# Two more dummy products, a constant made on VectorE, and one query transfer instead of two, in the opening of a fused attention and gated-FFN kernel

## Chip, cores, metric

One Trainium2 chip, one core. The metric is device time in microseconds, the median of several executions. The span in a profile is about 1.7 us shorter than the time of the same run.

## The reference, cut to what matters

```python
# attention: 4 batches, 8 heads, 768 tokens, head 64; window of +-15 tokens
k_sum = k.reshape(B, H, nb, 32, D).max(axis=3)       # one key per block of 32
v_sum = v.reshape(B, H, nb, 32, D).mean(axis=3)      # one value per block: "block means"
scores = [window scores | q . k_sum * scale + log(32)]
x = softmax(scores) @ [v | v_sum]                    # -> 3072 tokens x 512
# gated FFN with a gated residual
ffn = (gelu(x @ w_gate) * (x @ w_val)) @ w_out
out = x + sigmoid(x @ w_res) * ffn
```

## The kernel before

The work goes in eight units of 384 tokens. The opening: the first unit's keys and queries are loaded, turned on TensorE (PE), scored and normalised, while the FFN weights stream in behind them. Only the touched parts are shown.

```python
nc.vector.memset(warm[:], 0.0)
nc.vector.memset(ident[:], 0.0)
...
nc.vector.memset(bmean[:], 1.0 / BLK)                # block-mean constant, BLK = 32
...
nc.sync.dma_start(out=kf[:], in_=...)                # keys of pair 0, f32
nc.sync.dma_start(out=qf[:], in_=...)                # queries of pair 0, f32
load_tokens(kt, k, 0, 0, S, 2, 4)                    # GpSimd queue, casts on the way
select(ident[:], ALU.not_equal, 1.0, 0, -1, 1)
load_tokens(qa, q, 0, 0, TU, 2, 4)
for h in (4, 6):
    load_tokens(kt, k, 0, 0, S, h, h + 2)
    load_tokens(qa, q, 0, 0, TU, h, h + 2)
select(maskt[0:96], ...); select(maskt[0:96], ...)
load_values(0, NC); load_values(0, 0)
select(bias_t[96:128, :], ...)
for c in range(1, NC):
    load_values(0, c)
select(bmean[:], ALU.is_ge, 0.0, 32 * (NB + 94) - WIN, -32, 1)
select(bmean[:], ALU.is_ge, 0.0, 31 + WIN - 32 * (NB + 94), 32, -1)
for c in range(6):                                   # six pieces of each gate weight
    if c == 5:
        load_tokens(qb, q, 0, TU, S, 0, H)           # queries of the second unit
    nc.gpsimd.dma_start(out=w_gate[:, :, sl], in_=wg_src[:, :, sl])
    nc.gpsimd.dma_start(out=w_val[:, :, sl], in_=wv_src[:, :, sl])
...
def keep_warm(n, wp=None):                           # dummy products, result unused
    for i in range(n):
        nc.tensor.matmul(wp[:], warm[:, 0:128], warm[:], start=True, stop=True)
...
keep_warm(8, s1[0])
nc.scalar.copy(kt[:, 0]..., kf[:, 0])                # cast of the first keys
nc.vector.tensor_copy(kt[:, 1]..., kf[:, 1])
nc.vector.tensor_copy(qa[:, 0:2]..., qf[:])
t = k_first(0)                                       # 16 turns on PE, then an ACT copy
q_step(qa, 0, 0, TU, 0, *MM, nc.vector.tensor_copy)  # 8 turns
keep_warm(2, s1[0])
...
t = k_first(1)
q_step(qa, 0, 0, TU, 1, *MM)
k_first_rest(*t)                                     # VectorE: block maxima and copies
s = mask_into(s_tiles())
keep_warm(2, s1[0])
s_step(0, 0, st, s)                                  # first scores
```

The softmax here doesn't subtract the row's maximum and nothing guards it: scores larger than these inputs give would overflow.

Of the kernel before, what the change touches and what calls it, by code (L numbers as in the profile page):

```python
# [11 lines left out]
ALU = mybir.AluOpType  # L12
# [3 lines left out]
def kernel(  # L16
# [11 lines left out]
    nc = tc.nc  # L28
    B, H, S, D = q.shape
    assert (B, H, S, D) == (4, 8, 768, 64)  # L30
    BLK, WIN = 32, 16
    NB = S // BLK
# [9 lines left out]
    TU = S // 2  # L42
# [23 lines left out]
    ident = const.tile([128, 128], BF16, name="ident")  # L66
# [3 lines left out]
    bmean = const.tile([128, NB - 2 + 128], BF16, name="bmean")  # L70
# [14 lines left out]
    def token_tile(lo, hi, name):  # L85
        j = (hi - lo) // PP
        return qk1.tile([PP, H, j, D], BF16, tag=name, name=name)

    def load_tokens(t, src, b, lo, hi, h0, h1):
        j = (hi - lo) // PP  # L90
        nc.gpsimd.dma_start(
            out=t[:, h0:h1].rearrange("p h j d -> p h (j d)"),
            in_=src[b, h0:h1, lo:hi].rearrange("h (p j) d -> p h (j d)", j=j),
        )

    def load_values(b, c):

        lo, hi = (max(0, c * 128 - WIN), c * 128 + 128 - WIN) if c < NC else (S - WIN, S)
        dst = vext[b % 2][0 if c else WIN:128, 2 * c, :, 0:D] if c < NC else vext[b % 2][64:64 + WIN, NT - 1, :, 0:D]
        nc.gpsimd.dma_start(out=dst, in_=v[b, :, lo:hi, :].rearrange("h p d -> p h d"))  # L100
# [3 lines left out]
    with tc.manual_schedule():  # L104
# [13 lines left out]
        def select(ap, op, fill, base, step, cm):  # L118
            nc.gpsimd.affine_select(out=ap, in_=ap, compare_op=op, fill=fill, base=base,
                                    pattern=[[step, ap.shape[-1]]], channel_multiplier=cm)  # L120
# [2 lines left out]
        nc.vector.memset(ident[:], 0.0)  # L123
        nc.vector.memset(bias_t[:], 0.0)
        nc.vector.memset(bias_t[96:128, :], logblk)
        nc.vector.memset(bmean[:], 1.0 / BLK)
        nc.vector.memset(maskt[:], 1.0)
        vext_consts(0)
        kw_consts(0)
# [2 lines left out]
        kt, qa, qb = token_tile(0, S, "k0"), token_tile(0, TU, "qa"), token_tile(TU, S, "qb")  # L132
# [5 lines left out]
        load_tokens(kt, k, 0, 0, S, 2, 4)  # L138
        select(ident[:], ALU.not_equal, 1.0, 0, -1, 1)
        load_tokens(qa, q, 0, 0, TU, 2, 4)  # L140
        for h in (4, 6):
            load_tokens(kt, k, 0, 0, S, h, h + 2)
            load_tokens(qa, q, 0, 0, TU, h, h + 2)
        select(maskt[0:96], ALU.is_ge, 0.0, -1, -1, 1)
        select(maskt[0:96], ALU.is_ge, 0.0, 2 * WIN - 1, 1, -1)
        load_values(0, NC)
# [1 line left out]
        select(bias_t[96:128, :], ALU.is_ge, -30000.0, NB - 1, 0, -1)  # L148
        for c in range(1, NC):
            load_values(0, c)  # L150
        select(bmean[:], ALU.is_ge, 0.0, 32 * (NB + 94) - WIN, -32, 1)
        select(bmean[:], ALU.is_ge, 0.0, 31 + WIN - 32 * (NB + 94), 32, -1)

        wg_src = moe_w_gate.rearrange("(ko ki) f -> ki ko f", ki=128)
        wv_src = moe_w_val.rearrange("(ko ki) f -> ki ko f", ki=128)
# [61 lines left out]
        def q_step(src, b, lo, hi, hp, pool, tag, copy=nc.scalar.copy):  # L217
            tp = turn_pair(src, hp, pool, tag)
            copy(qT[b % 2][hp][:, lo:hi].rearrange("d (p j) -> d p j", j=tp.shape[2]), tp)
# [12 lines left out]
        def k_first_rest(tp, kw):  # L232
            ks = work.tile([128, NB], BF16, tag="ks", name="ks")
            nc.vector.tensor_reduce(out=ks[:], in_=tp.rearrange("d j (n w) -> d n j w", w=4),
                                    axis=mybir.AxisListType.XY, op=ALU.max)
            nc.vector.tensor_copy(kw[:, 0:HT, BLK0:BLK0 + NB], ks.unsqueeze(1).to_broadcast([128, HT, NB]))
            nc.vector.tensor_copy(kw[:, 1:HT, 0:WIN], kw[:, 0:HT - 1, OWN + QT - WIN:OWN + QT])
            nc.vector.tensor_copy(kw[:, 0:HT, POST:POST + WIN], kw[:, 1:HT + 1, OWN:OWN + WIN])
# [44 lines left out]
        def vsum_out(b, vs, h0, h1, copy):  # L283
            copy(vsum[b % 2][96:128, h0:h1, 0:D],
                 vs[96:128, h0 * D:h1 * D].rearrange("p (h d) -> p h d", d=D))

        def v_spread(b, c0, c1, part, copy=nc.vector.tensor_copy):

            V = vext[b % 2].rearrange("p (c e) h d -> p c e h d", e=2)
            if part == 0:  # L290
                copy(V[0:64, c0:c1, 1, :, 0:D], V[64:128, c0:c1, 0, :, 0:D])
            else:
                hi = min(c1, NC - 1)
                copy(V[64:96, c0:hi, 1, :, 0:D], V[0:32, c0 + 1:hi + 1, 0, :, 0:D])
# [10 lines left out]
        def s_tiles(two=None):  # L305
            if two:
                return [pool.tile([128, 512], F32, tag=tag, name="s1") for pool, tag in two]
            return ps_s.tile([128, 2, 512], F32, tag="s", name="s")

        def mask_into(s):  # L310
            two = isinstance(s, list)
            for hh in range(2):
                nc.tensor.matmul((s[hh] if two else s[:, hh])[:, 0:TU].rearrange("p (t q) -> p t q", t=HT), ident[:],
                                 nmask.unsqueeze(1).to_broadcast([128, HT, QT]),
                                 start=True, stop=False, skip_group_check=True)
            return s
# [128 lines left out]
        def keep_warm(n, wp=None):  # L445
            if wp is None:
                wp = ps_mm.tile([128, 512], F32, tag="mm", name="wp")
            for i in range(n):
                nc.tensor.matmul(wp[:], warm[:, 0:128], warm[:], start=True, stop=True)  # L449
# [18 lines left out]
        st = new_unit()  # L468
        nc.scalar.activation(pre[:], bias_t[0:1, :], AF.Exp)
        s1 = s_tiles((AO, TT))  # L470
        keep_warm(8, s1[0])
        nc.scalar.copy(kt[:, 0].rearrange("p j d -> p (j d)"), kf[:, 0])
        nc.vector.tensor_copy(kt[:, 1].rearrange("p j d -> p (j d)"), kf[:, 1])
        nc.vector.tensor_copy(qa[:, 0:2].rearrange("p h j d -> p h (j d)"), qf[:])
# [5 lines left out]
        t = k_first(1)  # L480
        q_step(qa, 0, 0, TU, 1, *MM)
        k_first_rest(*t)
        s = mask_into(s_tiles())
        keep_warm(2, s1[0])
        s_step(0, 0, st, s)
# [30 lines left out]
        vsum_sum(0, *MM, (5,), vs, first=False, last=True)  # L516
        keep_warm(1, wp)
        vsum_out(0, vs, 0, 2, nc.vector.tensor_copy)
        vsum_out(0, vs, 2, 8, nc.scalar.copy)
        for hp in range(NP):  # L520
            av_part(0, hp, st, blocks=True)
# [10 lines left out]
        for u in range(NU):  # L532
            b, half = u // 2, u % 2
            nb = b + 1
            n = u + 1
# [107 lines left out]
            if u == 1:  # L643
                k_rest(kW[1][3], nc.scalar.copy)
                v_spread(1, 0, HT // 2, 0)
                v_spread(1, 0, HT // 2, 1, nc.scalar.copy)
                end_step(u, st, 0)
                vs = vsum_sum(1, *SS, last=True)
                vsum_out(1, vs, 0, H, nc.scalar.copy)
                for hp in range(2):  # L650
                    vsum_bc(1, hp, 0, HT)
# [68 lines left out]
```

## Time and profile before

| | before |
|---|---|
| median of the first 3 runs (lowest, highest) | 257.66 us (257.52, 258.19) |
| the profiled run itself | 258.93 us, span 257.2 |
| PE busy | 97% of the span |
| first gate product of the first unit | 22.48 us |

The lines that carry the reading are in the prediction below.

In a timeline row the columns are start and duration in us, engine, line, operation, output<-inputs, shape, and in brackets the idle time before it and what ended that. Line numbers of the changed kernel are about ten higher from the middle of the file on (the dummies' L449 becomes L458).

### The profile page before, as it was taken

The page shows a single profiled execution, that of the slowest core. Times are in us where ns is not written, and L with a number is a line of the kernel's source. Part 1 is how long each engine was busy: PE and PEld are TensorE (multiplying, and loading weights), DVE is VectorE, ACT ScalarE, POOL GpSimd, SP SyncE. Part 2 cuts the span into 40 slices and gives each one's busy share as a digit, 9 for nine tenths or more (in the row PEclk, how much of TensorE's full clock was granted, in tenths as well). Part 3 has the DMA queues.
Part 4 walks back from the last instruction along what each step waited for, and adds up shares of the span by engine and source line. Part 5 has one row for each costly group of instructions (what it writes and reads, how often), then busy time and mean ns, then how long its engine had stood idle before and what let it go on. Part 6 is the DMA issues. An engine that isn't in the chain of part 4 may idle for free.

```text
span 257.2 us, 5751 instructions
## 1 busy us (share of the span) xinstructions
PE 250.6 (97%) x2240; PEld 139.8 (54%) x2240; DVE 172.6 (67%) x397; ACT 142.2 (55%) x249; POOL 103.5 (40%) x143
## 2 busy tenths in 40 slices
PE   7989999999999999999999999999999999999993
PEld 3445555566645555456654655556554655555543
DVE  4674975486487876779659768679568853764333
ACT  3584449645597536648683537458683537443310
POOL 7995533792979930028993560020001000010000
PEclk9999999999999999999999999999999999999999
DMA  7999999999999999759999999256003100130012
GB/s 152 157 144 195 197 204 201 149 172 150 128 152 172 168 149 159 109 136 148 162 129 151 183 154 131 49 143 120 0 3 88 82 3 1 33 138 3 0 41 83
DMA packets 118955, 30.46 MB, mean 118 GB/s; under 512 B 106064, under 2 KB 116752, under 8 KB 118928
## 3 DMA queue, kind: packets, MB, share of 16 engines
q0 software_dynamic: 86880, 19.90, 84.9%
q1 hardware_dynamic: 32048, 10.20, 25.2%
q8 instruction: 17, 0.28, 0.4%
q14 instruction: 10, 0.08, 0.1%
HBM read 32.51 MB, written 6.29 MB: 151 GB/s over the span
## 4 chain that ended last, share of the span: by engine, by line
PE 94%; ACT 2%; DMA 1%; DVE 1%; issue 0%; DVEq 0%
PE f L432 24%; PE vv L398 23%; PE g L398 22%; PE r L416 9%; PE gv L545 4%; PE ao L362 4%; PE s L330 3%; DMA kf<-in_k_dram 1%; PE xp L381 1%; PE vs L279 1%; PE s L449 1%; PE tp L226 1%; PE tp L195 1%; ACT kW L228 1%; PE gv L398 1%; PE tp L188 1%
## 5 line engine op out<-in xcount | busy, mean ns | idle before, releaser
L398 PE MATMUL vv<-xT,w_val 128*128 128x384 bf16 x360 | 73.7, 326 | 0.0
L404 ACT ACTIVATE ge<-g 128x384 f32<-128x384 f32 x85 | 41.8, 491 | 51.8 <-DVE gvT L405 25.9
L398 PE MATMUL g<-xT,w_gate 128*128 128x384 bf16 x340 | 69.7, 326 | 0.0
L405 DVE TENSOR_TENSOR gvT<-ge,vv 128x384 bf16<-128x384 f32 x90 | 49.2, 551 | 30.2 <-PE vv L398 26.9
L432 PE MATMUL f<-w_out,gvT 128*128 128x512 bf16 (+2 forms) x312 | 68.0, 363 | 0.0
L443 POOL DMA_DIRECT2D out_dram<-o x15 | 8.3, 552 | 100.4 <-DVE rz L370 81.9
L398 PEld LDWEIGHTS <-w_val 128*128 128x128 bf16 x364 | 35.6, 98 | 23.4
L398 PEld LDWEIGHTS <-w_gate 128*128 128x128 bf16 x344 | 33.3, 98 | 21.6
L432 PEld LDWEIGHTS <-gvT 128*128 128x128 bf16 x312 | 28.5, 98 | 28.9
L422 ACT ACTIVATE th<-r 128x512 f32<-128x512 f32 x24 | 14.2, 602 | 25.8 <-PE r L416 25.8
L437 DVE SCALAR_TENSOR_TENSOR th<-th,f 128x512 f32<-128x512 f32 (+2 forms) x26 | 16.7, 641 | 12.5 <-PE f L432 8.5
L416 PE MATMUL r<-w_res,xT 128*128 128x512 bf16 x96 | 24.4, 380 | 0.0
L175 POOL DMA_DIRECT2D k_sb<-in_k_dram x24 | 19.8, 836 | 11.2 <-DMA w_out<-in_moe_w_out_dram 5.2
L100 POOL DMA_DIRECT2D vext<-in_v_dram x28 | 23.6, 895 | 0.7 <-PE vv L398 0.7
L347 DVE TENSOR_TENSOR P<-P,maskt 128x768 bf16<-128x768 bf16 x28 | 15.5, 557 | 9.5 <-ACT P L336 5.0
L175 POOL DMA_DIRECT2D q_sb<-in_q_dram x24 | 19.8, 875 | 1.8 <-DMA k_sb<-in_k_dram 1.8
L372 DVE TENSOR_TENSOR xn<-ao,rz 128x384 bf16<-128x384 f32 x32 | 17.8, 557 | 1.1
L439 DVE SCALAR_TENSOR_TENSOR o<-th,xn 128x512 f32<-128x512 f32 (+2 forms) x26 | 16.9, 651 | 0.9
L336 ACT ACTIVATE P<-s,bias_t 128x384 bf16<-128x384 f32 x32 | 16.8, 578 | 1.1 <-PE s L330 1.1
L383 ACT COPY xT<-xp 128x384 bf16<-128x384 bf16 x17 | 7.9, 484 | 15.3 <-PE xp L381 15.3
L339 ACT ACTIVATE P<-s,bias_t 128x768 bf16<-128x768 f32 x16 | 14.5, 904 | 2.7 <-PE s L330 2.5
L175 POOL DMA_DIRECT2D v_sb<-in_v_dram x16 | 13.3, 925 | 0.0
(104 smaller groups left out, 248.9 us busy)
## 6 DMA issues: line engine op xcount, KB each, us to landing
out_dram<-o POOLq DMA_DIRECT2D x15, 256.0 KB, 2.4
vext<-in_v_dram POOLq DMA_DIRECT2D x20, 128.0 KB, 7.1
k_sb<-in_k_dram POOLq DMA_DIRECT2D x24, 96.0 KB, 7.8
q_sb<-in_q_dram POOLq DMA_DIRECT2D x24, 96.0 KB, 4.5
out_dram<-o SPq DMA_DIRECT2D x8, 256.0 KB, 3.8
w_gate<-in_moe_w_gate_dram POOLq DMA_DIRECT2D x6, 256.0 KB, 8.8
w_val<-in_moe_w_val_dram POOLq DMA_DIRECT2D x6, 256.0 KB, 9.1
w_out<-in_moe_w_out_dram POOLq DMA_DIRECT2D x3, 512.0 KB, 15.6
```

Of the source, the lines that this page charges most:

```text
L100: nc.gpsimd.dma_start(out=dst, in_=v[b, :, lo:hi, :].rearrange("h p d -> p h d"))
L175: nc.gpsimd.dma_start(out=sb[b][:, h // 2, :, h % 2 * D:h % 2 * D + D], in_=src[b, h].rearrange("(c p) d -> p c d", c=NC))
L336: nc.scalar.activation(P[:, hh].rearrange("p t q -> p (t q)"), s[hh][:, 0:TU], AF.Exp, scale=scale, bias=bias_t[:])
L347: nc.vector.tensor_mul(Pf, Pf, maskt.unsqueeze(1).to_broadcast([128, 2 * HT, QT]))
L372: nc.vector.tensor_mul(xn, ao[:, :, :, 0:D], rz.to_broadcast([128, NSUB, 2, D]))
L398: nc.tensor.matmul(acc[:, 0:TU], w[:, ko, fs], st["xT"][:, ko, :], start=(ko == 0), stop=(ko == KO - 1))
L404: nc.scalar.activation(ge[:], g[:, 0:TU], AF.Gelu)
L405: nc.vector.tensor_mul(gvT[:, fo, :], ge[:], vv[:, 0:TU])
L416: nc.tensor.matmul(r[:], st["xT"][:, ko, ss], w_res[:, ko, :], start=(ko == 0), stop=(ko == KO - 1))
L432: nc.tensor.matmul(st["f", sub][:, 0:c1 - c0], gvT[:, fo, ss], w_out[:, fo, c0:c1], start=(fo == 0), stop=(fo == FO - 1))
L437: nc.vector.scalar_tensor_tensor(th, th, 1.0, f[:, 0:c1 - c0], ALU.add, ALU.mult)
L439: nc.vector.scalar_tensor_tensor(o[:, 0:c1 - c0].rearrange("p (k d) -> p k d", d=128), th.rearrange("p (k d) -> p k d", d=128), 0.5, st["x ...
```

## The change

Two more dummies are to fill the idle time ahead of the first turn, so that PE's clock comes up sooner. Making the constant on VectorE and merging two transfers takes work off GpSimd, which issues the value and weight transfers.

```diff
-        nc.vector.memset(bmean[:], 1.0 / BLK)
+        nc.vector.memset(bmean[:], 0.0)
...
-        for h in (4, 6):
-            load_tokens(kt, k, 0, 0, S, h, h + 2)
-            load_tokens(qa, q, 0, 0, TU, h, h + 2)
+        load_tokens(kt, k, 0, 0, S, 4, 6)
+        load_tokens(qa, q, 0, 0, TU, 4, 8)
+        load_tokens(kt, k, 0, 0, S, 6, 8)
...
-        select(bmean[:], ALU.is_ge, 0.0, 32 * (NB + 94) - WIN, -32, 1)
-        select(bmean[:], ALU.is_ge, 0.0, 31 + WIN - 32 * (NB + 94), 32, -1)
...
+        def mean_consts():
+
+            c = NB + 93
+            with nc.allow_low_precision("sums of one element"):
+                for lo, hi, x in ((0, WIN, c), (WIN, 128 - WIN, c + 1), (128 - WIN, 128, c + 4)):
+                    n = (hi - lo + BLK - 1) // BLK
+                    nc.vector.tensor_reduce(out=bmean[:, x:x + n],
+                                            in_=ident[:, lo:hi].rearrange("p (n w) -> p n w", n=n),
+                                            axis=mybir.AxisListType.X, op=ALU.add)
+            nc.vector.tensor_scalar_mul(bmean[:, c:c + 5], bmean[:, c:c + 5], 1.0 / BLK)
...
-        keep_warm(8, s1[0])
+        keep_warm(10, s1[0])
...
         k_first_rest(*t)
+        mean_consts()
         s = mask_into(s_tiles())
```

## The prediction

> **What bounds the kernel now.** I read the page first: busy shares, then the chain that ended last, then the waits of the tensor engine (PE), then the timelines of the first 40 us engine by engine, because all three parts of the change sit there.
>
> The page's shares and the head of its chain:
>
> ```profile
> PE 250.6 (97%) x2240; PEld 139.8 (54%) x2240; DVE 172.6 (67%) x397; ACT 142.2 (55%) x249; POOL 103.5 (40%) x143
> ...
> PE 94%; ACT 2%; DMA 1%; DVE 1%; issue 0%; DVEq 0%
> ```
>
> PE is busy 97% of a span of 257.2 us. The list of PE's waits over the whole execution adds up to 2.5 us, and 1.3 of that is the start. From about 22.5 us, when the first gate products run, the chain of waits is PE alone without a gap. So only the first 22 us can give or take anything, and what moves there moves the end one for one, unless a later operand is late. I therefore need to know what sets the pace between 1.3 and 22 us. The timeline of PE for that stretch:
>
> ```profile
> 1.27 3.60 PE L449 MATMUL s<-warm 128*128 128x512 bf16 x8 [1.27 <-DVE warm L122]
> 5.20 0.85 PE L226 MATMUL tp<-ident,k 96*64 96x96 bf16 x16 [0.33 <-ACT k L472]
> 5.84 0.52 PE L195 MATMUL tp<-ident,qa 96*64 96x96 bf16 x8
> 6.30 1.03 PE L449 MATMUL s<-warm 128*128 128x512 bf16 x2
> 7.26 0.85 PE L226 MATMUL tp<-ident,k 96*64 96x96 bf16 x16
> 8.36 0.82 PE L313 MATMUL s<-nmask,ident 128*128 128x384 bf16 x2
> 8.98 1.06 PE L449 MATMUL s<-warm 128*128 128x512 bf16 x2
> 9.97 0.50 PE L330 MATMUL s<-qT,kW 64*128 64x64 bf16 x12
> 10.41 0.69 PE L449 MATMUL s<-warm 128*128 128x512 bf16 x2
> 11.36 0.53 PE L226 MATMUL tp<-ident,k 96*64 96x96 bf16 x16
> ```
>
> Columns are start, duration, engine, line, operation. Three things are to be seen. The eight dummy products (L449) end, in pace, at 1.27 + 8 x 0.427 = 4.69 us, and PE then stands idle until the key cast lets the first turn begin at 5.20. Second, the same work has two speeds: sixteen turns of keys occupy 0.85 us at 5.20 and 7.26 but 0.53 us at 11.36, and two dummies take 1.06 us at 8.98 and 0.69 at 10.41. PE runs at half speed until about 10.6 us and at full speed after. The page's row of granted clock shows 9 in every slice, so it does not show this; the durations do. Third, in the slow stretch the chain of waits is PE nearly without a break:
>
> ```profile
> 5.20 0.85 PE tp L226 x16
> 6.05 0.32 PE tp L195 x8
> 6.37 0.96 PE s L449 x2
> 7.33 0.78 PE tp L226 x15
> ...
> 11.91 0.02 issue
> 11.93 0.80 ACT kW L228
> ```
>
> After that it is ACT (key copy of pair 2, query copy, two exponentials, key copy of pair 3), VectorE (the maximum of pair 3) and PE again at 16.30. So the end depends on when ACT can begin the key copy of pair 2, now at 11.93 us, and PE's slow clock decides that.
>
> **What the Trainium skill says.** "TensorE: Matmul & The Clock Gate", Part 1, section "What's actually happening", says that PE starts at half clock, that a busy window of about 3413 ns releases it, and that the window runs free of the kernel's start. The trace agrees in speed (0.427 us a dummy early, about half that later) and in order: idle time spoils the stretch from 4.69 to 5.20, everything after 5.20 is dense, and the release comes at about 10.6. If the window's edges are at 10.6 minus multiples of 3.41, they are at 7.2 and 3.8: the window 3.8 to 7.2 held the gap of 0.51 us and did not release, the next one did. This is an inference; no view shows the edges. The same page, Part 4, says that turns do not count as busy in the same way; the window that released held 1.17 us of turns, so here they do not prevent it. "VectorE: DVE Perf Modes", section "Zero memsets can be issued as uint32 (trn2)", says a zero memset takes half the elements; the trace agrees (the 128x128 identity as 128x64 uint32 0.11 us, the 128x150 block-mean constant filled with 1/32 0.18 us). "DMA: Bandwidth & Descriptors", section "Rules for kernel authors", says to coalesce small transfers; here each issue costs GpSimd about 0.65 us, which the trace does show.
>
> **The change part by part.** The instruction order of the two builds differs only as the diff says: two products on PE, four small instructions on VectorE, and on GpSimd one transfer and two selects fewer.
>
> Dummies. Ten instead of eight end at 1.27 + 10 x 0.427 = 5.54 us, so the first turn starts 0.34 us later than 5.20 but without the gap. Taking the window edges of this trace, 3.8 to 7.2 now holds 1.74 us of dummies, 1.17 of turns and 0.5 of dummies, about the mix of the window that released, so full speed should come at about 7.2. Recomputed from there with durations of the fast stretch: turns of keys of pair 1 at about 7.4 (7.26 before; their load landed before that); the ACT copy 0.57 us after (11.36 to 11.93 in the fast stretch), at 7.97 instead of 8.16; masks and two dummies end at about 8.9. The first scores need the blocks of pair 0 from VectorE. They were there at 8.74, come 0.34 later because the first turn does, 9.08. So scores start at 9.08 instead of 9.97, and the exponential 0.42 us after (14.19 to 14.61), at 9.5 instead of 10.58; it ends at 10.4. PE goes on: scores 0.28, two dummies 0.43, masks 0.42 bring the turns of pair 2 to 10.21 instead of 11.36, and the key copy of pair 2 to 10.78 instead of 11.93. Gain 1.15 us. Everything from 11.93 to 22.5 is a chain of fixed durations behind this copy, so it keeps the gain if operands come.
>
> Constant. GpSimd loses two selects:
>
> ```profile
> 12.32 0.68 POOL L119 TENSOR_SCALAR_AFFINE_SELECT bmean<-bmean 128x150 bf16<-128x150 bf16 x2
> 12.96 0.77 POOL L160 DMA_DIRECT2D w_gate<-in_moe_w_gate_dram  x1
> ```
>
> so the weight issues start 0.66 us sooner. VectorE gains three sums over at most 96 elements and one scaling of five, at 0.1 to 0.2 us each (its reciprocal on six elements takes 0.20): about 0.6 us. They stand after the blocks of pair 1, where VectorE is idle:
>
> ```profile
> 12.76 0.96 DVE L234 TENSOR_REDUCE ks<-tp 128x24 bf16<-128x768 bf16 x1 [2.17 <-ACT kW L228]
> ```
>
> The idle time of 2.17 us shrinks to about 1.1 and still holds 0.6. The constant is first read at 14.90 (about 13.75 after). Cost on the path: 0.
>
> Queries. One issue fewer, about 0.65 us of GpSimd; the values and weights are issued that much sooner. The keys of pair 3 (landed at about 9.7 before, first turned at 12.70) and the queries of pairs 2 and 3 have over a microsecond in hand. By itself it is worth nothing on the path, but it and the selects protect the weights. The sixth piece of the value weights is issued at 24.67 and takes 11.5 us to land:
>
> ```profile
> w_val<-in_moe_w_val_dram POOLq DMA_DIRECT2D x1, 256.0 KB, 11.5
> ...
> 37.11 0.81 PE L398 MATMUL vv<-xT,w_val 128*128 128x384 bf16 x4
> ```
>
> It lands at 36.1 and is read at 37.11: 1.0 us in hand. If PE came 1.15 us sooner and the load no sooner, PE would wait 0.15. GpSimd now issues the weights 1.3 us sooner, but landings follow each other about 1.3 to 1.5 us apart, so the queue is limited by transfers, not by issues; I estimate the landings 0.6 us sooner, the share that comes from starting the values sooner. That leaves about 0.4 in hand.
>
> Sum: 1.15 gained by the clock, 0 by the other two: 257.66 - 1.15 = 256.5. I take off a little for the cases below: 256.6.
>
> **Rivals.** First, the clock is not released sooner: the turns do not count enough, or the threshold lies elsewhere. Then the later first turn remains, and the time is 257.66 + 0.3 = about 258.0. For it: the window that failed also held 1.17 us of turns. Against it: the window that released held as much, and the only clear difference is the gap. I give it 15%.
>
> Second, the release varies from run to run, since the windows run free of the start. With no gap allowed the release before falls anywhere from 5.20 + 3.41 = 8.6 to 12.0, and after from 1.27 + 3.41 = 4.7 to 8.1. The same recomputation with a release at 4.7 gives the key copy of pair 2 at about 10.2, a gain of 1.7; the three runs before, 0.67 us apart, fit such a lottery. This widens the range on both sides, 255.9 to 257.1.
>
> Third, the gain meets a new wait: the last weights, above, or VectorE's copies into the key blocks, which take up to 0.56 us beside GpSimd's value issues against 0.20 later. If landings do not move, the gain stops at about 1.0 us: 256.7. If a copy is slower by 0.4 us in the new position, the gain is 0.75: 256.9.
>
> Fourth, the issues alone count and the clock does not matter: then the gain would be 0, because no PE wait in the trace names a load after the start.
>
> **Range and chances.** From 255.9 (early release, no new wait) to 257.3 (a small gain, half of it lost in waits); the 15% of no release lies above it. 2% is 5.15 us; the stretch that the change touches could give at most about 2 us, and could lose at most about 0.5. So within 2% at 0.98.
>
> **What would show it.** The ten dummies end at about 5.5 with no idle before the first turn; turns at 7.3 to 7.5 take about 0.53 us instead of 0.85; the key copy of pair 2 starts at 10.2 to 10.9; the first scores wait for VectorE; GpSimd's first weight issue is at about 11.6; VectorE still has idle time before the maximum of pair 2; PE has no wait for weights at about 36 us. Wrong would be: turns at 7.4 still at 0.85 us, a wait for the last weights, or VectorE's new sums ending after the key copy of pair 2.

## The result

| | before | changed |
|---|---|---|
| median (lowest, highest), 4 runs each | 257.63 us (257.52, 258.19) | 257.12 us (257.03, 257.39) |
| span of the profiled run | 257.2 | 255.3 |

The ratio is 0.9978 with a 95% interval of 0.9961 to 0.9995. Ratios here are the mean time of one kernel's runs over that of the other's of the same rounds, so not quite the ratio of the medians. The median moved by 0.51 us, to a time inside the stated range; the central forecast, 256.6 us, asked for about twice that. The two profiles differ by 1.9 us, almost four times as much. That mismatch is what the experiments had to explain.

The page of the changed kernel, shares and head of the chain:

```profile
PE 247.1 (97%) x2216; PEld 138.9 (54%) x2242; DVE 173.1 (68%) x401; ACT 142.2 (56%) x249; POOL 102.4 (40%) x140
...
PE 91%; POOL 3%; DMA 2%; issue 1%; DVE 1%; ACT 0%; POOLq 0%; DVEq 0%
```

GpSimd (POOL) has entered the chain with 3%, and DMA has risen from 1% to 2%. The timeline of PE in the opening:

```profile
1.27 3.84 PE L458 MATMUL s<-warm 128*128 128x512 bf16 x10 [1.27 <-DVE warm L122]
5.05 0.53 PE L224 MATMUL tp<-ident,k 96*64 96x96 bf16 x16
...
6.33 0.53 PE L224 MATMUL tp<-ident,k 96*64 96x96 bf16 x16
...
8.41 0.35 PE L339 MATMUL s<-qT,kW 64*128 64x64 bf16 x12 [0.37 <-DVE kW L236]
...
9.56 0.53 PE L224 MATMUL tp<-ident,k 96*64 96x96 bf16 x16
...
12.64 0.35 PE L339 MATMUL s<-qT,kW 64*128 64x64 bf16 x12 [0.72 <-DVE kW L236]
```

Even the first turns, at 5.05, take 0.53 us: PE is at full speed there, not from 7.2 us on as predicted. The ten dummies take 3.84 us, less than ten at 0.427 us would, so the last of them already ran fast. The trace also keeps a record of the granted clock, which begins at 4.4 us here and at 10.6 us in the kernel before; nothing is recorded ahead of that, and the page's clock row counts it as full. I call a run early or late by that moment; the turns' 0.53 or 0.85 us show it too.

PE waits twice for VectorE's copies into the key blocks, 0.37 and 0.72 us (0.7 us in all before). The chain of waits no longer runs through PE's turns but through the issue and the landing of a value piece (issued at 9.14, used at 15.47):

```profile
9.14 6.29 DMA vext<-in_v_dram
15.43 0.04 issue
15.47 0.38 PE vs L277
```

VectorE's timeline has the new constant in its idle time, as predicted; three sums and a scaling are over by 10.04 (0.86 us of work, where 0.6 was predicted), and 0.92 us are still idle:

```profile
9.15 0.34 DVE L291 TENSOR_REDUCE bmean<-ident 128x1 bf16<-128x16 bf16 x3
9.52 0.52 DVE L294 TENSOR_SCALAR bmean<-bmean 128x5 bf16<-128x5 bf16 x1
10.96 0.96 DVE L232 TENSOR_REDUCE ks<-tp 128x24 bf16<-128x768 bf16 x1 [0.92 <-ACT kW L226]
```

And the sixth weight pieces are used at 34.69 (gate) and 35.34 us (value), without a wait, but with little in hand: the value piece landed at 35.2 by the trace.

```profile
34.69 0.82 PE L407 MATMUL g<-xT,w_gate 128*128 128x384 bf16 x4
35.34 0.81 PE L407 MATMUL vv<-xT,w_val 128*128 128x384 bf16 x4
```

### The profile page after: what moved, and what is told of

The parts are those of the page before. It is cut to its first block, busy times and chain, and to the rows that moved or that the text cites. A ratio compares the mean times of both kernels' runs of the same rounds, so it can differ in the third digit from the quotient of the medians.

```text
span 255.3 us, 5730 instructions
## 1 busy us (share of the span) xinstructions
PE 247.1 (97%) x2216; PEld 138.9 (54%) x2242; DVE 173.1 (68%) x401; ACT 142.2 (56%) x249; POOL 102.4 (40%) x140
## 4 chain that ended last, share of the span: by engine, by line
PE 91%; POOL 3%; DMA 2%; issue 1%; DVE 1%; ACT 0%; POOLq 0%; DVEq 0%
PE f L441 24%; PE vv L407 23%; PE g L407 22%; PE r L425 8%; PE gv L555 4%; PE ao L371 4%; PE s L339 3%; DMA vext<-in_v_dram 2%; PE xp L390 1%; POOL vext L100 1%; PE vs L277 1%; POOL k L91 1%; PE gv L407 1%; PE tp L186 1%; POOL qa L91 0%
## 5 line engine op out<-in xcount | busy, mean ns | idle before, releaser
L441 PE MATMUL f<-w_out,gvT 128*128 128x512 bf16 (+2 forms) x298 | 66.0, 362 | 0.8 <-issue 0.2
L407 PEld LDWEIGHTS <-w_gate 128*128 128x128 bf16 x344 | 33.3, 98 | 21.6
L381 DVE TENSOR_TENSOR xn<-ao,rz 128x384 bf16<-128x384 f32 x32 | 17.8, 558 | 1.1
L448 DVE SCALAR_TENSOR_TENSOR o<-th,xn 128x512 f32<-128x512 f32 (+2 forms) x26 | 16.9, 651 | 0.9
```

Source lines behind the costliest of these rows:

```text
L381: nc.vector.tensor_mul(xn, ao[:, :, :, 0:D], rz.to_broadcast([128, NSUB, 2, D]))
L407: nc.tensor.matmul(acc[:, 0:TU], w[:, ko, fs], st["xT"][:, ko, :], start=(ko == 0), stop=(ko == KO - 1))
L441: nc.tensor.matmul(st["f", sub][:, 0:c1 - c0], gvT[:, fo, ss], w_out[:, fo, c0:c1], start=(fo == 0), stop=(fo == FO - 1))
L448: nc.vector.scalar_tensor_tensor(o[:, 0:c1 - c0].rearrange("p (k d) -> p k d", d=128), th.rearrange("p (k d) -> p k d", d=128), 0.5, st["x ...
```

## The experiments

Twelve series ran in three calls (e, f and g); each call's series share a chip and 11 runs of the kernel before. "Old loads" are those of the kernel before, "new loads" have the constant and the merged queries. All results were correct.

**Ten dummies alone** (e1).

```diff
-        keep_warm(8, s1[0])
+        keep_warm(10, s1[0])
```

> The kernel before with ten dummies instead of eight, nothing else. Theory A (the dummies give the gain, because a gapless stretch from 1.27 to 5.5 us lets the clock be released one window sooner in most runs): about 0.5 us faster than before, ratio 0.998, like the whole change. Theory B (the gain is GpSimd's: earlier values and weights; the clock is a lottery that the dummies hardly move): ratio 1.000 within 0.001, or 0.1 to 0.3 us slower where the first turn waits for the tenth dummy.

Measured: 258.06 us (257.44 to 258.82), before 257.88; ratio 0.9992 (0.9955 to 1.0029). No gain is seen, though the interval is wide enough to hold the whole change's 0.9978. The profile shows where an early start can be lost. The run was early (4.9 us), and its first gate product came at 20.69 us, as early as in the changed kernel (20.72). But at the sixth weight pieces PE waited, 0.17 and 0.50 us:

```profile
34.89 0.82 PE L398 MATMUL g<-xT,w_gate 128*128 128x384 bf16 x4 [0.17 <-DMA w_gate<-in_moe_w_gate_dram]
36.22 0.82 PE L398 MATMUL vv<-xT,w_val 128*128 128x384 bf16 x4 [0.50 <-DMA w_val<-in_moe_w_val_dram]
```

**New loads, eight dummies** (e2): the changed kernel with

```diff
-        keep_warm(10, s1[0])
+        keep_warm(8, s1[0])
```

> The changed kernel with eight dummies again: constant and queries only. Theory A: no gain, 257.6 us. Theory B: the whole gain, about 257.1 us. If both count it lies between.

Measured: 257.05 us, ratio 0.9967 (0.9931 to 1.0003). A gain as large as that of the whole change shows without the two dummies; alone it is not quite clear of 1, and g3 below repeats it. One of its six runs took 258.77 us; the other five 256.90 to 257.35.

**The constant alone** (e3) and **the queries alone** (e4): those parts of the diff, nothing else.

> The kernel before with the constant made by VectorE, nothing else. The selects stood behind the value issues, so values come no sooner and weights at most 0.6 us sooner; PE does not wait for weights in the profile before. Theory A: 257.6 us, no change within 0.1. Theory B: 0.1 to 0.2 us of gain at the most.

> The kernel before with the queries of pairs 2 and 3 in one transfer, nothing else. One issue fewer on GpSimd ahead of the values, so the values are issued about 0.5 us sooner. Theory A: no change within 0.1 us. Theory B: this is the part that gains, 0.3 to 0.5 us, since the chain of the changed kernel runs through the landing of a value piece at 15.4 us.

Measured: 257.35 us, ratio 0.9975 (0.9939 to 1.0011), and 257.40 us, ratio 0.9974 (0.9939 to 1.0010). Each looks as good as both, and neither is clear of 1. The control below shows why such single series cannot part 0.2 from 0.5 us. The profile of e3 was a late run (10.4 us, 258.90 us by the clock), that of e4 an early one (5.3 us, 257.59). In e4 the values did not land sooner, against what I expected: PE waited 0.47 us for a value piece at 15.96.

**The kernel before, once more** (f1), as a control.

> The kernel before itself, as a control and for a second look at its profile. The profiles so far fall into two kinds by the moment at which PE's turns become fast: late (about 10.5 us: before, 258.93 us by the clock of the runs, and the constant alone, 258.9 us) and early (4.4 to 6.5 us: the four others, 257.0 to 258.2). If the release is a lottery with eight dummies, about 3 runs in 4 are early: a time of about 257.6 us in most runs, about 258.8 in the rest, ratio 1.000 within 0.003. Theory B (loads bind the early runs) expects an early profile of this kernel to show PE waiting for the sixth weight pieces near 35 us. Theory A (dummies decide the gain) expects all its runs late or mixed, with no such wait.

Measured: 258.40 us (257.36 to 259.06), against 257.73 in the 11 shared runs of the very same kernel; ratio 1.0021 (0.9999 to 1.0043). So a series of six can be off by 0.2% through the draw of runs alone: four of these six lie above 258.3, one of the eleven does. The profile fell on a late run again (9.6 us, 258.45 us), which left no early profile of this very kernel; ten dummies with old loads stand in for it. Its turns, from its timeline of PE:

```profile
5.38 0.85 PE L226 MATMUL tp<-ident,k 96*64 96x96 bf16 x16 [0.52 <-ACT k L472]
...
7.45 0.85 PE L226 MATMUL tp<-ident,k 96*64 96x96 bf16 x16
```

**The changed kernel, once more** (f2).

> The changed kernel itself, on the same chip as the control. Theory A and B both: about 257.1 us. If ten dummies secure the early release, none of its runs lies above 258.4; if not, about one in four does.

Measured: 257.29 us (257.02 to 257.78), ratio 0.9982 (0.9967 to 0.9998), none above 258.3. The gain is reproduced. Its profile is an early run (6.8 us).

**New loads without any dummy ahead of the first turn** (f3).

```diff
-        keep_warm(10, s1[0])
```

> The changed kernel without any dummy ahead of the first turn: the first turn starts at about 5.1 us, and no full busy window can end before about 8 us, so all runs are late. Expected 1.0 to 1.5 us slower than the changed kernel, 258.2 to 258.6 us, with turns of pair 1 still at 0.85 us. If the clock were not what parts the two kinds of run, it would be as fast as the changed kernel.

Measured: 258.35 us, all five runs between 258.18 and 258.48; against f2 that is 1.06 us. The profile is late (10.3 us), with slow turns:

```profile
4.98 0.85 PE L224 MATMUL tp<-ident,k 96*64 96x96 bf16 x16 [4.98 <-ACT k L480]
...
7.04 0.85 PE L224 MATMUL tp<-ident,k 96*64 96x96 bf16 x16
```

So the lead of dummies as such is worth about 1 us with the new loads, and late runs are the cost of missing it. It is for the ninth and tenth that no gain was seen.

**GpSimd slowed ahead of the weights** (f4): the changed kernel with a new tile `scratch`, which VectorE fills once (not shown), and

```diff
         for c in range(1, NC):
             load_values(0, c)
+        for _ in range(4):
+            select(scratch[:], ALU.is_ge, 0.0, 32 * (NB + 94) - WIN, -32, 1)   # unused tile
```

> The changed kernel with four selects on an unused tile between the value issues and the weight issues: about 1.36 us of GpSimd, as much as constant and queries together had saved ahead of the weights, everything else as changed. Theory B, in the form that the moment of issue counts: about 0.5 us slower than the changed kernel, with PE waiting for weights near 35 us. If the transfers alone set the landings, less than 0.2 us, since landings follow each other 1.3 us apart and an issue in hand waits anyway.

Measured: 257.50 us, ratio 0.9993 (0.9973 to 1.0012), against 257.29 and 0.9982 of the changed kernel: 0.2 us, between the two expectations and not clear of noise. The profile says more. The first weight piece was issued at 13.16 us instead of 11.73 and landed, by the trace, at 18.03 instead of 17.94. So 1.43 us in the issue moved that landing by 0.1 (in f2 the same piece, issued at 11.67, landed only at 18.79): at that point transfers set the landings, not issues. No wait for weights appears. The sixth value piece landed at 35.65, against 35.2 and 35.5 in the two profiles of the changed kernel.

**Old loads without dummies ahead** (g1).

> The kernel before (old loads, constant by GpSimd) without any dummy ahead of the first turn. All runs late, as in the new-loads kernel without dummies, which took 258.35 us (258.18 to 258.48). If the loads act only where PE is early (a wait for weights or values), it takes about the same, 258.2 to 258.6 us. If issuing sooner helps by itself, 258.8 to 259.1.

Measured: 259.70 us (258.67 to 260.05), ratio 1.0069 (1.0033 to 1.0106) to a before of 257.40. Both expectations missed: it is slower than either. The list of PE's waits names a new one, far from the opening:

```profile
PE gv L544 <- DMA xT<-xn: 1.2, 1, 1.2
```

It is at 143.29 us in the timeline: PE waits for the tokens of a later unit, which are turned by a DMA. That turn took up to 6.6 us to land in this window, and at most 5.6 in the same window of the kernel before, where the third of these turns landed at 142.7, about in time. In f3, late too but with new loads, the wait is absent. What delays that turn was not tested; this run does show that the late part of the kernel has hardly any slack either. The highest times of the kernel before (259.37, 259.74 and 260.18 us) may be of this kind, but no profile fell on one.

**Ten dummies, old loads, again** (g2).

> The kernel before with ten dummies, again. Early in all runs, but held by the sixth weight pieces near 35 us, as its first profile showed (waits of 0.17 and 0.50 us): 257.6 to 258.0 us, 0.4 to 0.7 us over the next two. If its first series (258.06) was only noise, about 257.2 us.

Measured: 257.86 us (257.52 to 258.51), ratio 1.0006 (0.9970 to 1.0041). Again no gain. Its early profile (5.7 us) waits 0.3 us for a value piece and 0.1 for the sixth value weights.

**New loads, eight dummies, again** (g3).

> The changed kernel with eight dummies, again: most runs about 257.1 us, one in four at 258.3 to 258.8 (late). The lowest time of the series equals that of the changed kernel within 0.2 us, 256.9 to 257.1.

Measured: 257.01 us, all six runs between 256.90 and 257.29, ratio 0.9971 (0.9937 to 1.0005). This time no late run. Its profile is early (5.6 us) with eight dummies and an idle gap ahead of the first turn:

```profile
1.26 3.59 PE L458 MATMUL s<-warm 128*128 128x512 bf16 x8 [1.26 <-DVE warm L122]
5.07 0.77 PE L224 MATMUL tp<-ident,k 96*64 96x96 bf16 x16 [0.21 <-ACT k L481]
...
6.55 0.53 PE L224 MATMUL tp<-ident,k 96*64 96x96 bf16 x16
```

The first turns straddle the release, the next are fast. The gap did not prevent it.

**Ten dummies, old loads, late queries split** (g4): the kernel before with ten dummies and

```diff
-                load_tokens(qb, q, 0, TU, S, 0, H)
+                load_tokens(qb, q, 0, TU, S, 0, H // 2)
             nc.gpsimd.dma_start(out=w_gate[:, :, sl], ...)
             nc.gpsimd.dma_start(out=w_val[:, :, sl], ...)
+        load_tokens(qb, q, 0, TU, S, H // 2, H)
```

> Ten dummies and the old loads, but the late queries in two halves, the second half issued after the sixth weight pieces: these pieces then have 192 KB less ahead of them and should land about 0.7 to 1.0 us sooner. If the wait for them is what eats the early start, it is 0.4 to 0.6 us faster than ten dummies alone, about 257.2 us, and its profile has no wait for weights above 0.1 us. If not, the same as ten dummies alone.

Measured: 257.64 us (256.67 to 258.06), ratio 0.9987 (0.9948 to 1.0027), against 257.86 and 1.0006 of ten dummies alone. The wait is gone and the sixth value piece landed at 35.4 instead of 36.2:

```profile
35.22 0.82 PE L399 MATMUL g<-xT,w_gate 128*128 128x384 bf16 x4
35.88 0.81 PE L399 MATMUL vv<-xT,w_val 128*128 128x384 bf16 x4
```

In the profile the first product with the residual weights, which ends this stage, started at 38.94 us against 39.3 in both profiles of ten dummies alone: 0.36 us sooner. In the times it is 0.2 us, half of what I expected and inside the noise. Nor is this kernel faster than the kernel before (257.40 us): that removing the wait gains time is seen in the profile alone.

**All profiles side by side**, times in us from the traces; "idle" is PE's idle time between the dummies and the first turn, as the brackets of its timeline give it:

| loads, dummies ahead | idle | clock released | first gate product | 6th value weights landed | first residual product | span |
|---|---|---|---|---|---|---|
| old, 8 (before) | 0.33 | 10.6 | 22.5 | 36.1 | 40.2 | 257.2 |
| old, 8 (f1) | 0.52 | 9.6 | 22.2 | 36.4 | 39.8 | 256.7 |
| old, 0 (g1) | no dummies | 10.8 | 22.5 | 36.1 | 40.2 | 258.4 |
| old, 10 (e1) | none | 4.9 | 20.7 | 36.2 | 39.3 | 256.4 |
| old, 10 (g2) | none | 5.7 | 21.3 | 36.2 | 39.3 | 256.3 |
| old but queries split, 10 (g4) | none | 6.9 | 21.3 | 35.4 | 38.9 | 255.9 |
| constant only, 8 (e3) | 0.68 | 10.4 | 22.5 | 35.7 | 40.3 | 257.2 |
| queries only, 8 (e4) | 0.24 | 5.3 | 21.5 | 35.1 | 39.2 | 255.9 |
| new, 0 (f3) | no dummies | 10.3 | 22.3 | 34.7 | 40.0 | 256.7 |
| new, 8 (e2) | 0.26 | 6.5 | 21.0 | 34.7 | 38.7 | 255.6 |
| new, 8 (g3) | 0.21 | 5.6 | 20.8 | 34.6 | 38.5 | 255.2 |
| new, 10 (changed) | none | 4.4 | 20.7 | 35.2 | 38.4 | 255.3 |
| new, 10 (f2) | none | 6.8 | 21.6 | 35.5 | 39.3 | 256.1 |
| new, GpSimd slowed, 10 (f4) | none | 5.4 | 20.8 | 35.7 | 38.9 | 255.4 |

Two things are to be read from it. Late runs reach the residual product at 39.8 to 40.3 whichever the loads: there PE is behind its operands, and sooner loads buy nothing in this stage. Early runs reach it at 39.3 with old loads and at 38.4 to 39.3 with new ones: in e1 and g2 the old loads' weights, which land at 36.1 to 36.4 in all five profiles with unsplit queries, hold PE back. How much can be read from the time between the two products: it is 17.7 to 17.8 us in eleven of the profiles, 18.6 in e1 and 18.0 in g2. (In f4 it is 18.1, with a wait for VectorE and none for weights.) So the wait costs 0.9 and 0.3 us there; the rest of the differences at the residual product is the moment of the first gate product, which follows the clock.

One thing more is in the table. The six profiles with eight dummies part by the idle time ahead of the first turn: 0.21, 0.24 and 0.26 us in the three early ones, 0.33, 0.52 and 0.68 in the three late ones. With ten dummies there is no idle time, and all six are early. Three of these lines, of e2, e4 and e3:

```profile
5.12 0.85 PE L224 MATMUL tp<-ident,k 96*64 96x96 bf16 x16 [0.26 <-ACT k L481]
...
5.10 0.62 PE L226 MATMUL tp<-ident,k 96*64 96x96 bf16 x16 [0.24 <-ACT k L472]
...
5.54 0.85 PE L224 MATMUL tp<-ident,k 96*64 96x96 bf16 x16 [0.68 <-ACT k L481]
```

The first turn waits for the cast of the first keys, and the cast for their landing: it began at 4.40 to 4.45 us in the three early profiles and at 4.53 to 4.87 in the late ones. So what looks like a draw goes with the landing of one load. Six profiles show it and no experiment moved that load, so it is an association.

## Why the prediction was right in number and wrong in cause

The measured 257.12 us lies in the range 255.9 to 257.3 and the forecast of "within 2%" held. The sum behind it did not: that the number fits is luck, since a gain of another origin, 0.51 us and not 1.15, fell inside a wide range.

**The step that failed first: "Taking the window edges of this trace".** The 1.15 us of gain were computed from one profile, and that profile was a late run: 258.93 us against a median of 257.66. With eight dummies the release changes from run to run. Of the six profiles with eight dummies three were late and three early; of 43 timed runs of the kernel before, 11 lie above 258.3 us. So the typical run before was, by its time, already early, and the dummies could give it little; this is inferred, since both profiles of this very kernel are late. The prediction named this draw as its second rival but placed a release before at 8.6 to 12.0 us, "with no gap allowed". That premise is refuted: e2 and g3 were released at 6.5 and 5.6 us with a gap of 0.26 and 0.21 us in view, and the changed kernel at 4.4, ahead of the earliest moment that the prediction allowed (4.7). That a gap can hold the release back was a sound idea; what was missed is that a short one does not, and that most runs before were, by their times, early already.

The Trainium skill's page "TensorE: Matmul & The Clock Gate" says in the same section, Part 1, "What's actually happening": "For modeling, the ramp penalty is <1% of a typical kernel span; don't fit to a specific cold count." The runs agree: about 1 us of 257 between f3 and f2, and a release that moves from run to run. I fitted to one count.

**The dummies: 1.15 us predicted, no gain measured.** Four series carry both load parts: 0.9967 and 0.9971 with eight dummies, 0.9978 and 0.9982 with ten. Two carry ten dummies and old loads: 0.9992 and 1.0006. By the intervals of these two, their mean is known to about 0.7 us (an estimate): 1.15 us is excluded, half a microsecond is not. New loads with eight dummies beat old loads with ten by 1.01 (e2, e1) and 0.85 us (g3, g2) in the medians. All six profiles of kernels with ten dummies were early, so ten may well make late runs rarer. The timed runs do not settle it: above 258.3 us lie 14 of 67 runs with eight dummies and 3 of 34 with ten, in kernels of several loads. The mark is rough, too: two of the five runs of f3, which has no dummies ahead, lie below it.

**Constant and queries: 0 predicted, the gain measured.** The step "By itself it is worth nothing on the path" was right for the late run that it was read from and wrong for early runs. There PE is ready for the sixth value weights at 35.7 (e1) and 36.1 us (g2), and the old loads land them at 36.2. What I had as the third rival, the weights, was then not a limit on the change but a limit on the kernel before. Shown are the gain of the new loads without the two dummies (e2, g3), the waits of e1 and g2, their absence with new loads, and their absence with the split of g4. Not shown is the wait in the kernel before itself, of which no early profile exists; g4's times, too, leave it open.

**How the loads come sooner was mis-stated.** I estimated the landings 0.6 us sooner because the values start sooner. The last value piece landed later, not sooner (by the trace at 17.3 us against 16.8; over all profiles 16.8 to 18.0 with old loads and 16.9 to 18.2 with new ones), and f4 shows that the moment of issue hardly moves the first weight. From about 20 us on GpSimd itself sits idle until earlier weight pieces have landed, before the change and after it, so the time saved ahead is gone by the sixth pieces:

```profile
24.67 0.74 POOL L161 DMA_DIRECT2D w_val<-in_moe_w_val_dram  x1 [1.31 <-DMA w_gate<-in_moe_w_gate_dram]
...
23.29 0.76 POOL L158 DMA_DIRECT2D w_gate<-in_moe_w_gate_dram  x1 [1.74 <-DMA w_val<-in_moe_w_val_dram]
```

The first line is of the kernel before, the second of the changed one. Yet the sixth piece lands 0.7 to 1.6 us sooner than at 36.2 in all five profiles with new loads, and 0.5 sooner in f4. Between the first and the sixth piece the old loads lose time in steps of about 2 us where 1.3 is the rule; the new loads have fewer of these. Why is open, and so is the share of each of the two parts.

**What held.** The step from the clock to the time: for a release at 4.7 us the prediction gave the key copy of pair 2 at about 10.2 and a gain of 1.7 us, and with a release at 4.4 the copy began at 10.13 and the first gate product came 1.76 us sooner than in the late profile before. VectorE's sums are hidden; the fast turns take 0.53 us; PE is dense to the end after the opening; the first scores wait for VectorE's blocks, as foreseen. The chance of 15% for "no release sooner" was put on the wrong event: the release came, and most runs, by their times, already had it.

None of the experiments beats the changed kernel clearly; its loads with eight dummies tie with it (257.01 and 257.05 us).

## What to carry to other kernels

Before reasoning from a profile, compare the profiled run's own time with the median: where it is off by more than the effect you look for, the profile shows another kind of run. Where the kinds part, look just ahead of the parting for something that differs, here the idle time ahead of the first turn. Then ask for each part of a change in which kind of run it is on the path. For effects of 0.2%, run the unchanged kernel as one of the experiments: here that control alone came out at 1.0021.

## What the Trainium skill lacked or had wrong

- "TensorE: Matmul & The Clock Gate", Part 1, gives a busy window of about 3.4 us but no share of it that must be busy. In all 14 profiles the stretch at full clock lasts 72, 73 or 74 times 3.413 us (245.76 in the kernel before, 249.17 in the changed one), so I count windows of that length back from the release. By this estimate every window that released the clock held at most 0.32 us without work on PE (the changed kernel's, 0.95 to 4.36 us), and every one that did not held at least 0.33 (the kernel before's, 3.80 to 7.21 us).
- The same page, Part 4, says of turns that they do not count as busy in the same way. With the same windows, the one that released the clock in f1 (6.2 to 9.6 us) held 1.5 us of turns and so at most 1.9 us of other products, while one of the kernel before (0.4 to 3.8 us) held 2.5 us of dummies and did not release it. By this estimate turns count.
- No page tells of the single long step in a row of like transfers: seven value pieces land about 1 us apart, but in every profile the longest step takes 1.4 to 3.2 us (12.35 to 14.46 us in the changed kernel), not always at the same place.
- "DMA: Bandwidth & Descriptors" gives no time for a DMA turn beside ordinary loads; one took 2.3 us alone and 4.3 to 6.6 us beside the loads of a later batch (g1, near 107 and 140 us).
